# Five engine programs emitted straight into the main body, with no block around them

## The chip, the cores and the metric

The kernel runs on one core of a Trainium2 chip. The metric is device time in microseconds of one execution, as a median of several runs. Each run also has a profile with a *span*: the time from the first to the last recorded instruction of the program. Time minus span is what the execution spends outside the program's own records, before the first and after the last of them. That difference gets a short name here: the *outside time*. Spans of timed runs are given to 0.1 us, so a single outside time is good to about 0.05 us.

The granted clock is the share of its full clock that TensorE was given; it was at least 0.99 in every run quoted, every one of them undisturbed. Ratios and their 95% intervals are those of the record: mean times of fast runs of the same rounds, where some sets enter without their first run, so they are not quite the ratio of the medians or means quoted beside them. Instants to the nanosecond are read from the trace's single records; the views shown here round them to 0.1 or 0.01 us.

## The reference, cut to what matters

```python
def reference(A_x, A_wqkv, A_wo, B_x, B_w_gate, B_w_up, B_w_down, gate_w):
    x = A_x                                             # [1, 2048, 640] bf16
    g = _sigmoid((x * gate_w).sum(-1, keepdims=True))
    a = _A_ref(x, A_wqkv, A_wo)                         # linear attention, 32 heads of 20
    b = _B_ref(x, B_w_gate, B_w_up, B_w_down)           # gelu(x@w_gate) * (x@w_up) @ w_down
    return g * a + (1 - g) * b
```

The change does not touch the arithmetic. What matters is that the work is one long stream of matrix products, followed by the store of the last 128 rows of the result.

## The kernel before

The kernel plans all operations first. Each engine (TensorE `pe`, ScalarE `act`, VectorE `dve`, GpSimd `pool`, SyncE `sp`) has a list of operations with the semaphores (counters by which one engine waits for another or for a transfer) that each waits for. At the end the lists are emitted, one body per engine, inside a block.

```python
    def emit(self, eng, handle):
        for (waits, fn, key, inc) in self.ops[eng]:
            for (k, v) in waits:
                handle.wait_ge(self.sems[k], v)
            inst = fn(handle)
            inst.then_inc(self.sems[key], inc)
# ... (cut)
    with (
        nc.Block() as block,
        nc.sbuf_tensor("pool", [128, TOTAL], BF16) as pool,
# ... (cut: semaphores, tiles, the plan of all operations)
            n_out = P.count["out"]

            @block.sync
            def _(sp):
                P.emit("sp", sp)
                sp.wait_ge(s_out, n_out)      # all output transfers have landed

            @block.tensor
            def _(pe):
                P.emit("pe", pe)
# ... (cut: the same for scalar, vector, gpsimd)
```

The block does two things. Each engine branches into a body of its own and, behind it, to a common end: in the program as built there are ten unconditional branches, two on each engine. When the block is left, all five engines meet in a closing barrier. Each engine drains (a record that, on VectorE, ends just behind the engine's last operation) and reports on one semaphore, GpSimd collects the reports, and then it releases the others. The opening of the program also has such a barrier, which does not belong to the block.

The last tile's output goes out in two transfers, so that the first 512 columns leave while the last 128 are still computed:

```python
                    if end:
                        P.op("sp", lambda e, c0=c0, cn=cn: e.dma_start(
                            out[0, i * 128:(i + 1) * 128, c0:c0 + cn], out_sb[i][:, c0:c0 + cn]),
                            reads=[r_out[i] if n == 0 else r_out_b[i]], dma="out")
```

Of the kernel before, what the change touches and what calls it, by code (L numbers as in the profile page):

```python
# [159 lines left out]
def bass_gated_mix__linear_attn_block__geglu_ffn__prompt_kernel(  # L160
# [59 lines left out]
    n_dma_in = 100  # L220

    with (
        nc.Block() as block,
        nc.sbuf_tensor("pool", [128, TOTAL], BF16) as pool,
        nc.psum_tensor("ps", [128, 8, 512], F32) as ps,
        nc.semaphore("s_pe") as s_pe,
# [5 lines left out]
        with contextlib.ExitStack() as stack:  # L232
            dma_sems = [stack.enter_context(nc.semaphore("s_in%d" % i)) for i in range(n_dma_in)]

            P = _Plan(["pe", "act", "dve", "pool", "sp"])
# [240 lines left out]
            for n in range(2 * NT):  # L476
# [6 lines left out]
                if n == 3:  # L483
                    dma_in(wq[:, :, 0:640], A_wqkv[:, 0:640].rearrange("(k p) w -> p k w", p=128), [r_wq],
                           eng="act")
# [285 lines left out]

            n_out = P.count["out"]

            @block.sync
            def _(sp):
                P.emit("sp", sp)
                sp.wait_ge(s_out, n_out)

            @block.tensor
            def _(pe):  # L780
                P.emit("pe", pe)

            @block.scalar
            def _(act):
                P.emit("act", act)

            @block.vector
            def _(dve):
                P.emit("dve", dve)

            @block.gpsimd
            def _(g):
                P.emit("pool", g)


# [26 lines left out]
```

## Time and profile before

| kernel before, first three runs | |
|---|---|
| time, median | 278.12 us (277.77 to 278.28) |
| profiled run: time, span | 277.85 us, 275.927 us |
| outside time of that run | 1.92 us |
| TensorE busy | 270.1 us, 98% of the span |
| from the start of the last matmul to the end of the last record | 2.660 us |
| from the start of the record that waits for the outputs to the end of the last record | 0.397 us |

These lines of the profile's page give the span, the busy time of the engines (PE is TensorE) and the chain of waits that ended last, by engine:

```profile
span 275.9 us, 4048 instructions
...
PE 270.1 (98%) x1663; PEld 140.4 (51%) x1696; DVE 138.5 (50%) x233; ACT 78.3 (28%) x132; POOL 26.1 (9%) x28
...
PE 95%; DMA 2%; issue 1%; ACTq 1%; DVE 0%
```

TensorE is the bound. A change that leaves its stream alone can act only at the two ends.

The head, from the timeline (columns: start, duration, engine, line, operation, operands; a q behind an engine's name is its instruction queue):

```profile
0.80 0.57 ACTq L331 DMA_DIRECT2D pool<-in_gate_w_dram  x1
...
0.81 0.14 PEld L387 LDWEIGHTS ps<-const-bfloat16-1.0 128*128 128x128 bf16 x2 [0.81 <-issue]
...
3.72 1.28 ACT L441 ACT_TABLE_LOAD   x1 [3.72 <-issue]
```

The opening barrier releases the engines at 0.724 to 0.736 us, and the own work of all but VectorE, which first waits for TensorE until about 4.1 us, starts at 0.80 to 0.81 us. There is no room for anything long between the two.

The tail, as the view of the block's own source line. Columns are the line, engine, operation and count, then the shortest, median and longest duration in ns, then the first and last start in us:

```profile
L223 POOLq EVENT_SEMAPHORE  x2: 17/17/17, 275.7 to 275.8; - x2
L223 POOLq DRAIN  x1: 1512/1512/1512, 165.7 to 165.7; - x1
L223 ACTq DRAIN  x1: 826/826/826, 214.0 to 214.0; - x1
L223 PEldq DRAIN  x1: 1995/1995/1995, 271.5 to 271.5; - x1
L223 DVEq DRAIN  x1: 391/391/391, 273.5 to 273.5; - x1
L223 SPq COMPARE_BRANCH  x1: 38/38/38, 275.5 to 275.5; - x1
L223 SPq DRAIN  x1: 13/13/13, 275.7 to 275.7; - x1
L223 SPq EVENT_SEMAPHORE  x1: 17/17/17, 275.9 to 275.9; - x1
L223 ACTq EVENT_SEMAPHORE  x1: 17/17/17, 275.9 to 275.9; - x1
L223 DVEq EVENT_SEMAPHORE  x1: 21/21/21, 275.9 to 275.9; - x1
L223 PEldq EVENT_SEMAPHORE  x1: 51/51/51, 275.9 to 275.9; - x1
```

This is the whole closing barrier. GpSimd has drained at 167 us and ScalarE at 215 us, TensorE at 273.5 us and VectorE at 273.9 us, and all of them then sit and wait. SyncE arrives last: its wait for the outputs is carried by a compare-and-branch that starts at 275.530 us, and its drain follows at 275.706. Then GpSimd collects and releases, and at about 275.9 us all four others leave the barrier.

### The profile page before, as it was taken

The numbers are of one execution on the slowest core, as the hardware profiler recorded it, in microseconds if no ns is written. First come the engines' busy times: TensorE is split into PE (matmuls) and PEld (weight loads), VectorE is DVE, ScalarE is ACT, GpSimd is POOL, SyncE is SP. The second block draws the span as 40 slices with busy tenths as digits, with TensorE's granted clock in tenths as the row PEclk, the third lists the DMA queues.
The fourth block names the chain that finished last, engine by engine and source line by source line (L and its number), as shares of the span: only waits on it lengthen the run. The fifth ranks groups of instructions, "written<-read, shape, count | busy, mean of one in ns | idle before, by whom it ended". The sixth has DMA issues, their size and how long they took to land.

```text
span 275.9 us, 4048 instructions
## 1 busy us (share of the span) xinstructions
PE 270.1 (98%) x1663; PEld 140.4 (51%) x1696; DVE 138.5 (50%) x233; ACT 78.3 (28%) x132; POOL 26.1 (9%) x28
## 2 busy tenths in 40 slices
PE   8899999999999999999999999999999999999996
PEld 5455555555545444444444444444555555555553
DVE  2398888510234324999999998535000122212223
ACT  1355555210431454223222223224555100000000
POOL 5000000000000401242432422000000000000000
PEclk9999999999999999999999999999999999999999
DMA  7998997002120111122121221380000010111111
GB/s 178 172 199 238 395 402 244 12 6 44 23 48 21 50 46 54 25 46 48 26 49 24 47 50 24 60 309 14 0 0 2 24 47 26 48 50 48 50 48 48
DMA packets 36400, 22.38 MB, mean 81 GB/s; under 512 B 25759, under 2 KB 34975, under 8 KB 36383
## 3 DMA queue, kind: packets, MB, share of 16 engines
q1 hardware_dynamic: 34997, 20.49, 27.4%
q10 hardware_dynamic: 1386, 1.64, 2.2%
q8 instruction: 13, 0.21, 0.3%
q14 instruction: 4, 0.03, 0.0%
HBM read 13.11 MB, written 2.62 MB: 57 GB/s over the span
## 4 chain that ended last, share of the span: by engine, by line
PE 95%; DMA 2%; issue 1%; ACTq 1%; DVE 0%
PE ps L596 41%; PE ps L739 20%; PE ps L702 6%; PE ps L432 6%; PE ps L503 6%; PE ps L419 5%; DMA pool<-in_A_wqkv_dram 2%; PE ps L505 2%; PE ps L433 2%; PE ps L703 2%; PE ps L420 2%; PE ps L571 2%; PE ps L723 1%; ACTq L331 1%; PE ps L617 1%
## 5 line engine op out<-in xcount | busy, mean ns | idle before, releaser
L596 PE MATMUL ps<-pool 128*128 128x512 bf16 x509 | 113.0, 379 | 0.6
L596 PEld LDWEIGHTS ps<-pool 128*128 128x128 bf16 x520 | 50.4, 98 | 60.0 <-issue 0.3
L739 PE MATMUL ps<-pool 128*128 128x128 bf16 (+1 forms) x407 | 56.6, 297 | 0.6 <-issue 0.2
L604 DVE TENSOR_TENSOR pool<-ps,pool 128x512 bf16<-128x512 f32 x52 | 35.8, 688 | 33.6 <-PE ps L596 30.4
L602 ACT ACTIVATE pool<-ps 128x512 f32<-128x512 f32 x52 | 31.1, 597 | 72.5 <-PE ps L596 72.1
L750 DVE SCALAR_TENSOR_TENSOR pool<-ps,pool 128x512 bf16<-128x512 f32 (+1 forms) x32 | 16.2, 547 | 63.8 <-PE ps L739 63.8
L739 PEld LDWEIGHTS ps<-pool 128*128 128x128 bf16 x416 | 31.8, 98 | 25.3 <-issue 1.1
L648 POOL TENSOR_TENSOR pool<-pool 128x640 f32<-128x640 bf16 x16 | 22.5, 1409 | 140.1 <-DMA pool<-z_row 87.1
L441 ACT ACTIVATE pool<-ps 128x640 bf16<-128x640 f32 x32 | 22.3, 704 | 23.1 <-PE ps L420 13.5
L454 DVE SCALAR_TENSOR_TENSOR pool<-ps,pool 128x640 bf16<-128x640 f32 x32 | 26.4, 825 | 2.2
L656 DVE TENSOR_TENSOR pool<-pool 128x640 bf16<-128x640 bf16 x16 | 23.0, 1441 | 0.6
L419 PE MATMUL ps<-pool 128*128 128x512 bf16 x77 | 21.9, 383 | 0.7 <-DMA pool<-in_A_wqkv_dram 0.7
L432 PE MATMUL ps<-pool 128*128 128x512 bf16 x77 | 21.4, 379 | 0.0
L702 PE MATMUL ps<-pool 128*128 128x512 bf16 x77 | 21.3, 379 | 0.0
L503 PE MATMUL ps<-pool 128*128 128x512 bf16 x76 | 21.2, 379 | 0.0
L505 PE MATMUL ps<-pool 128*128 128x129 bf16 x80 | 17.6, 220 | 0.2
L420 PE MATMUL ps<-pool 128*128 128x128 bf16 x80 | 17.6, 220 | 0.2
L433 PE MATMUL ps<-pool 128*128 128x129 bf16 x80 | 17.6, 220 | 0.2
L703 PE MATMUL ps<-pool 128*128 128x128 bf16 x80 | 17.5, 219 | 0.2
L707 ACT ACTIVATE pool<-ps,pool 128x640 f32<-128x640 f32 x16 | 12.7, 794 | 9.2 <-PE ps L703 9.2
L451 DVE TENSOR_SCALAR pool<-pool 128x640 bf16<-128x640 bf16 x32 | 10.4, 325 | 7.4 <-ACT pool L441 5.8
L419 PEld LDWEIGHTS ps<-pool 128*128 128x128 bf16 x80 | 7.9, 98 | 10.2 <-DMA pool<-in_A_wqkv_dram 1.0
(51 smaller groups left out, 130.7 us busy)
## 6 DMA issues: line engine op xcount, KB each, us to landing
out_dram<-pool SPq DMA_DIRECT2D x15, 160.0 KB, 1.8
pool<-in_B_w_gate_dram SPq DMA_DIRECT2D x1, 2080.0 KB, 13.6
pool<-in_B_w_up_dram SPq DMA_DIRECT2D x1, 2080.0 KB, 18.3
pool<-in_A_x_dram SPq DMA_DIRECT2D x1, 1280.0 KB, 8.3
pool<-in_B_w_down_dram SPq DMA_DIRECT2D x1, 1120.0 KB, 6.0
pool<-in_A_wo_dram SPq DMA_DIRECT2D x6, 160.0 KB, 8.8
pool<-in_B_w_down_dram SPq DMA_DIRECT2D x1, 960.0 KB, 8.5
pool<-in_A_wqkv_dram ACTq DMA_DIRECT2D x5, 160.0 KB, 4.4
```

Source lines behind the costliest of these rows:

```text
L419: e.matmul(ps[:, b0, :], lhs, wk[:, k, 0:512], start=(k == 0), stop=(k == KC - 1))
L420: last = e.matmul(ps[:, b1, 0:128], lhs, wk[:, k, 512:640], start=(k == 0), stop=(k == KC - 1))
L432: e.matmul(ps[:, b0, :], lhs, wq[:, k, 0:512], start=(k == 0), stop=(k == KC - 1))
L433: last = e.matmul(ps[:, b1, 0:129], lhs, wq[:, k, 512:641], start=(k == 0), stop=(k == KC - 1))
L454: P.op("dve", lambda e: e.scalar_tensor_tensor(dst, ps_flat[:, b0 * 512:b0 * 512 + 640], 1.0 + EPS, e_buf[m], ALU.add, ALU.max), reads=[ba ...
L503: e.matmul(ps[:, bs[n], :], lhs, x_aug[:, i, 0:512], start=(i == 0), stop=(i == NT - 1))
L505: last = e.matmul(ps[:, bt, n * 129:(n + 1) * 129], lhs, x_aug[:, i, 512:641], start=(i == 0 and n == 0), stop=(i == NT - 1), skip_group_c ...
L596: last = e.matmul(ps[:, b, :], w[:, k, fc * 128:(fc + 1) * 128], xT[:, k, j * 512:(j + 1) * 512], start=(k == 0), stop=(k == KC - 1))
L602: P.op("act", lambda e: e.activation(ge[n], ps[:, gb, :], ACT.Gelu_apprx_tanh), reads=[bank[gb]], writes=[r_ge[n]])
L604: P.op("dve", lambda e: e.tensor_tensor(hT[fc][:, j * 512:(j + 1) * 512], ps[:, ub, :], ge[n], ALU.mult), reads=[bank[ub], r_ge[n]], write ...
L702: e.matmul(ps[:, b0, :], lhs, w2[:, m, 0:512], start=(m == 0), stop=(m == KC - 1))
L739: last = e.matmul(dst, lhs, wd[:, fc, c0:c0 + cn], start=False, stop=(fc == NFC - 2), skip_group_check=True)
```

## The change

The intent is to save the branches and the closing barrier: the programs synchronise by their own semaphores, and SyncE waits for the last output anyway.

```diff
     with (
-        nc.Block() as block,
         nc.sbuf_tensor("pool", [128, TOTAL], BF16) as pool,
...
-            @block.sync
-            def _(sp):
-                P.emit("sp", sp)
-                sp.wait_ge(s_out, n_out)
-
-            @block.tensor
-            def _(pe):
-                P.emit("pe", pe)
-
... (cut: the same for scalar, vector, gpsimd)
+            for eng, handle in (("sp", nc.sync), ("pe", nc.tensor), ("act", nc.scalar),
+                                ("dve", nc.vector), ("pool", nc.gpsimd)):
+                P.emit(eng, handle)
+            nc.sync.wait_ge(s_out, n_out)
```

More of the change, by code (lines that the diff above doesn't have):

```diff
@@ L772, in bass_gated_mix__linear_attn_block__geglu_ffn__prompt_kernel @@
             n_out = P.count["out"]
-            @block.sync
-            def _(sp):
-                P.emit("sp", sp)
-                sp.wait_ge(s_out, n_out)
-            @block.tensor
-            def _(pe):
-                P.emit("pe", pe)
-            @block.scalar
-            def _(act):
-                P.emit("act", act)
-            @block.vector
-            def _(dve):
-                P.emit("dve", dve)
-            @block.gpsimd
-            def _(g):
-                P.emit("pool", g)
+            for eng, handle in (("sp", nc.sync), ("pe", nc.tensor), ("act", nc.scalar),
+                                ("dve", nc.vector), ("pool", nc.gpsimd)):
+                P.emit(eng, handle)
+            nc.sync.wait_ge(s_out, n_out)
 _INS = ['A_x', 'A_wqkv', 'A_wo', 'B_x', 'B_w_gate', 'B_w_up', 'B_w_down', 'gate_w']
```

## The prediction

> What bounds the kernel now. The page's busy table has TensorE at 270.1 of 275.9 us (98%); the next, VectorE, at 50%. The chain that ended last is 95% TensorE, 2% DMA (the key weights at the start). The granted clock is 1.000. So the matmul stream from about 3 us to 273.5 us sets the time, with a short head and tail. The change alters no instruction of that stream: each engine keeps its program, waits and order. Only what stands around the five programs goes.
>
> The head. The trace shows an opening barrier that belongs to the program's start, not to the block: the engines are released at 0.724 to 0.736 us. It stays. From the end of that release to the engine's first own instruction it is 24 ns on TensorE (0.787 to 0.811), 56 ns on ScalarE's queue (0.745 to 0.801), 68 ns on SyncE's queue (0.741 to 0.809). No branch is recorded there. The Trainium skill, "Advanced Engine Details and Errata", section Control Flow Timing, gives about 51 ns for a branch; TensorE's 24 ns leave no room for one, so the branches to the bodies are probably laid out as fall-through. Estimated gain: 0 to 0.05 us, on the path, since the chain starts with ScalarE's weight issues at 0.80 us.
>
> The tail. The last matmul ends at about 273.5, VectorE's last eviction at 273.88; the last output transfer is issued at 273.95 to 274.39. SyncE's wait for the outputs ends at 275.530, recorded as a compare-and-branch of 38 ns that carries the wait. Then comes the block's barrier: SyncE's drain at 275.706 (138 ns behind the branch), GpSimd's collecting wait 275.744, its release 275.823, the other four engines' waits, the last ending at 275.927. The other drains came long before (VectorE's ended at 273.93), so only SyncE's arrival counts. From 275.530 to 275.927 is 0.397 us, all on the path, since nothing runs beside it. In its place stands one plain semaphore wait, 17 ns like SyncE's others. Gain in the span: 0.38 us.
>
> Outside the span. Timed run and span differ by 277.85 - 275.9 = 1.95 us. The Trainium skill, "Runtime: NRT & Kernel Launch", section on the preamble and postamble, says that the runtime puts its own barrier behind each kernel (about 1.5 us); no trace here shows it. It waits for SyncE in either version, so I expect 1.95 us to stay, perhaps a tenth or two less because four engines arrive early.
>
> Predicted time: 278.12 - 0.38 - about 0.04 = 277.7 us; a gain of 0.15%, within the spread of three runs (277.77 to 278.28). Range 277.2 to 278.2. Faster by over 2%: 1%. Within 2%: 98%. Slower by over 2%: 1%.
>
> What would show it. Right: a span of 275.5 +- 0.15; no drain, compare-and-branch or barrier wait behind the last output; all engines' busy times within 0.2 us; the first weight issue still at about 0.80 us. Wrong at the head: first issues more than 0.1 us earlier. Wrong at the tail: the time falls with no change of span, or the span falls and the time does not, so that the runtime's end absorbs the barrier.
>
> What would make it wrong. ScalarE's table load (1.283 us, now at 3.72, behind the weight issues) might be placed differently when all programs share one body: ahead of the issues it would delay the first weights by up to 1.3 us, still under 1%. The compiler could also attach waits to other instructions.

## The result, and the profile after

| first comparison, six runs each | before | after |
|---|---|---|
| time, median | 278.06 us (277.73 to 279.41) | 277.12 us (276.67 to 277.30) |
| ratio, 95% interval | | 0.9957 [0.9936, 0.9979] |
| span of the profiled run | 275.927 us | 275.882 us |
| outside time of the profiled run | 1.92 us | 1.31 us |
| last matmul's start | 273.267 us | 273.608 us |
| from there to the end of the last record | 2.660 us | 2.274 us |

The kernel is 0.94 us faster by the medians: within 2%, as forecast, but more than twice the gain that I had given it, and 0.08 us under the lower end of my range. At the same time the two profiled spans are almost equal. The two traces explain why, once three pieces are kept apart.

*The body.* The page's lines are as before, with 11 records fewer, which are the block's barrier and branch less the new wait:

```profile
span 275.9 us, 4037 instructions
...
PE 269.3 (98%) x1663; PEld 139.6 (51%) x1696; DVE 138.4 (50%) x233; ACT 78.2 (28%) x132; POOL 26.0 (9%) x28
...
PE 95%; DMA 2%; issue 1%; ACTq 1%; DVE 0%
```

From the first query matmul to the last matmul of the kernel the trace of before has 244.641 us, that of after 244.641 us. In all sixteen traces it lies between 244.639 and 244.642 us. The change does nothing there.

*The head.* It starts as before, and the table load did not move:

```profile
0.80 0.57 ACTq L330 DMA_DIRECT2D pool<-in_gate_w_dram  x1
...
0.81 0.14 PEld L386 LDWEIGHTS ps<-const-bfloat16-1.0 128*128 128x128 bf16 x2 [0.81 <-issue]
...
3.72 1.28 ACT L440 ACT_TABLE_LOAD   x1 [3.72 <-issue]
```

But the first query matmul starts at 28.626 us before and at 28.967 us after, 0.34 us later. The waits view says what TensorE waited for (total us, number of waits, longest). Before:

```profile
PEld ps L419 <- DMA pool<-in_A_wqkv_dram: 1.0, 1, 1.0
PE ps L419 <- DMA pool<-in_A_wqkv_dram: 0.7, 1, 0.7
```

After:

```profile
PEld ps L418 <- DMA pool<-in_A_wqkv_dram: 1.6, 1, 1.6
PE ps L418 <- DMA pool<-in_A_wqkv_dram: 1.3, 1, 1.3
```

In this run the key weights landed later, and TensorE waited 1.3 us for them in place of 0.7. The matmul behind this wait starts at 9.04 us before and at 9.38 us after, which is the whole 0.34 us. Is that an effect of the change? Subtract each kernel's traced tail (below) from the spans of its timed runs: what is left, the start of the last matmul, is 273.74 us on average in 42 runs with the block and 273.66 us in 68 runs of all kernels without it (standard errors 0.09 and 0.07). It spreads over more than 2 us in either group, so a difference of 0.34 us between two runs is within chance, and no effect of the block on the head is seen. The stretches of the windows view (columns: stretch, its length, then busy us of PE, PEld, DVE, ACT and POOL with counts, clock, DMA share, GB/s) locate it. Before:

```profile
0.00:10.00 10.00, 8.44 (x49) 4.65 (x50) 1.56 (x4) 1.28 (x1) 3.60 (x12) 1.00 0.88 183
10.00:70.00 60.00, 59.53 (x434) 33.94 (x441) 37.21 (x68) 24.29 (x50) 0.00 (x0) 1.00 0.65 187
...
273.00:276.00 3.00, 0.49 (x9) 0.31 (x6) 0.88 (x2) 0.00 (x0) 0.00 (x0) 0.98 0.18 55
```

After:

```profile
0.00:10.00 10.00, 7.29 (x47) 3.70 (x48) 1.56 (x4) 1.28 (x1) 3.59 (x12) 1.00 0.90 175
10.00:70.00 60.00, 59.53 (x434) 33.91 (x441) 37.21 (x68) 24.28 (x50) 0.00 (x0) 1.00 0.66 188
...
273.00:276.00 3.00, 0.83 (x14) 0.65 (x12) 1.08 (x2) 0.00 (x0) 0.00 (x0) 1.00 0.18 55
```

TensorE's busy time differs in the first 10 us (1.15 us less after) and in the last 3, where five matmuls more are left to do; between 10 and 70 us it is the same to the last digit, and so it is between 70 and 273 us (201.62 us in both).

*The tail.* The only record of the change's own last line is SyncE's wait:

```profile
L776 SPq EVENT_SEMAPHORE  x1: 17/17/17, 275.9 to 275.9; - x1
```

The tail is 0.386 us shorter, as predicted (0.38). It vanishes in the span because the head of this one run came 0.341 us later.

So the predicted saving is there, and what I missed lies elsewhere: outside the span, where 1.92 us had become 1.31. All six timed runs of after have 1.27 to 1.34 us.

### The profile page after: what moved, and what is told of

The parts are those of the page before. It is cut to its first block, busy times and chain, and to the rows that moved or that the text cites. A ratio compares the mean times of both kernels' runs of the same rounds, so it can differ in the third digit from the quotient of the medians.

```text
span 275.9 us, 4037 instructions
## 1 busy us (share of the span) xinstructions
PE 269.3 (98%) x1663; PEld 139.6 (51%) x1696; DVE 138.4 (50%) x233; ACT 78.2 (28%) x132; POOL 26.0 (9%) x28
## 4 chain that ended last, share of the span: by engine, by line
PE 95%; DMA 2%; issue 1%; ACTq 1%; DVE 0%
PE ps L595 41%; PE ps L738 20%; PE ps L431 6%; PE ps L701 6%; PE ps L502 6%; PE ps L418 5%; DMA pool<-in_A_wqkv_dram 2%; PE ps L504 2%; PE ps L432 2%; PE ps L702 2%; PE ps L419 2%; PE ps L570 2%; PE ps L722 1%; ACTq L330 1%; PE ps L616 1%
```

## The experiments

Three theories for the 0.6 us outside the span:

- A, own ends: behind its last instruction each engine has an end of its own that no record shows. An engine that is done early goes through it while the others still work. The closing barrier holds all five back until 275.9 us, and then the longest of the five ends counts.
- B: the barrier's drains and semaphore instructions themselves leave something behind the last record.
- C: the block's branches do.

All kernels below gave correct results. Each was timed beside runs of the kernel before on the same chip; the four sets (e, f, g, h) ran on four different chips, on which the kernel before had 1.87, 1.94, 1.93 and 1.96 us outside. Quoted are means over the runs, with the range of the single runs for the outside time.

### The noise, and the barrier put back in three ways

`e0_before_again` is the kernel before, unchanged.

> The kernel before, unchanged, to have its span beside each time. The time outside the span (timed run minus span) was 1.92 us in its one profiled run; the changed kernel's six runs have 1.27 to 1.34. All theories: 1.9 to 2.0 us in every run here, span 275.6 to 276.5 (it moves with the landing of the first weights), ratio 1.000 +- 0.001. If this gap moves by 0.3 us between runs, the 0.6 us that is unexplained was chance.

`e1_barrier_no_block` has a barrier, but no block:

```diff
             nc.sync.wait_ge(s_out, n_out)
+            nc.all_engine_barrier()
```

> The changed kernel with one all-engine barrier (drains and semaphores) put back behind SyncE's last wait, still no block and no branch. Theory A (the runtime's end begins on each engine when that engine is done, and the barrier holds all five back until 275.9): gap 1.9 to 2.0 us, tail from last matmul to last record about 2.65 us less SyncE's branch, ratio 0.999 to 1.000. Rival C (the branches of the block, at the head before the first record or at the end behind the last one, cost the 0.6 us): gap 1.3 us, time about 277.5.

`e2_all_wait_no_barrier` has neither, but all five engines end at the same time:

```diff
             nc.sync.wait_ge(s_out, n_out)
+            nc.tensor.wait_ge(s_out, n_out)
+            nc.scalar.wait_ge(s_out, n_out)
+            nc.vector.wait_ge(s_out, n_out)
+            nc.gpsimd.wait_ge(s_out, n_out)
```

> The changed kernel in which the four other engines also wait for the last output, each for itself: no barrier, no drain, no branch, but all five come to their end at the same time. Theory A (late arrival of the other engines at the runtime's end): gap 1.8 to 2.0 us with a tail about 0.38 us shorter than before, so ratio about 0.9985, time 277.6 to 277.7. Rival B (the barrier's own drains and semaphore instructions leave 0.6 us behind the last record): gap 1.3 us, time as the changed kernel's, ratio 0.996.

`e3_sem_barrier_no_block` has the barrier without drains:

```diff
             nc.sync.wait_ge(s_out, n_out)
+            nc.all_engine_barrier(sem_only=True)
```

> As e1, with the barrier made of semaphores alone, without drains. Theory A: gap 1.9 to 2.0 us as in e1, since the engines are as late; tail within 0.2 us of e1's. Rival B in the form 'the drains cost it': gap 1.3 us here and 1.9 in e1.

| run (6 runs each) | ratio to before, 95% | mean time | mean span | outside time | tail in the trace |
|---|---|---|---|---|---|
| before, in the same rounds (11) | | 278.22 | 276.35 | 1.87 (1.74 to 1.99) | |
| e0_before_again | 1.0013 [0.9987, 1.0039] | 278.55 | 276.67 | 1.88 (1.80 to 1.98) | 2.660 |
| e1_barrier_no_block | 1.0002 [0.9975, 1.0030] | 278.25 | 276.37 | 1.89 (1.71 to 1.98) | 2.555 |
| e2_all_wait_no_barrier | 1.0002 [0.9979, 1.0025] | 278.24 | 276.30 | 1.93 (1.78 to 2.07) | 2.325 |
| e3_sem_barrier_no_block | 0.9986 [0.9963, 1.0008] | 277.79 | 275.88 | 1.91 (1.77 to 2.06) | 2.483 |

The tail is from the start of the last matmul to the end of the last record. e0 shows the noise: its spans run from 275.7 to 277.7 us, while its outside times stay within 0.2 us. Therefore the verdict rests on the outside time and the tail, and not on the ratios, whose intervals are as wide as the effect. Some expectations missed for the same reason: e0's runs did not all lie in the stated 1.9 to 2.0 us and 275.6 to 276.5 us, and e2 was expected at 277.6 to 277.7 us and a ratio of 0.9985, but had 278.24 us and 1.0002. Its outside time (1.93 us) and its tail (0.34 us shorter than before) were about as theory A had them.

Theory C falls by e1: with no branch at all the outside time is back at 1.89 us. Theory B falls by e2 and e3: without barrier and drains, with nothing but one wait per engine for the last output, it is 1.93 us; with semaphores alone, 1.91. What the three have in common is that all engines end late, as three of e2's five waits show (SyncE, GpSimd, TensorE):

```profile
L776 SPq EVENT_SEMAPHORE  x1: 17/17/17, 276.3 to 276.3; - x1
...
L780 POOLq EVENT_SEMAPHORE  x1: 17/17/17, 276.3 to 276.3; - x1
...
L777 PEldq EVENT_SEMAPHORE  x1: 51/51/51, 276.3 to 276.3; - x1
```

e2 also shows that this does not pass through the span: its tail is only 0.05 us longer than after's, and its outside time 0.6 us.

SyncE's branch at the end does have a small cost, in the span. Here are e1's wait for the outputs, and the lines of its barrier that answer to SyncE's drain and last wait in the view of before:

```profile
L776 SPq EVENT_SEMAPHORE  x1: 17/17/17, 275.8 to 275.8; - x1
L777 SPq DRAIN  x1: 13/13/13, 275.8 to 275.8; - x1
L777 SPq EVENT_SEMAPHORE  x1: 17/17/17, 276.0 to 276.0; - x1
```

In e1 SyncE's wait starts at 275.769 us and its drain at 275.833, 64 ns later. Before, with the branch between them, it was 275.530 to 275.706, 176 ns (169 in e0). The branch at the end cost 112 ns; the tails differ by 0.105 us. The Trainium skill, "Advanced Engine Details and Errata", section Control Flow Timing, gives about 108 ns for a compare-and-branch; this trace agrees, although the record itself shows only 38 ns.

### One engine late beside SyncE

In each of these four runs one more engine waits for the last output, for instance:

```diff
             nc.sync.wait_ge(s_out, n_out)
+            nc.tensor.wait_ge(s_out, n_out)
```

> The changed kernel with SyncE and TensorE both waiting for the last output; ScalarE, VectorE and GpSimd end early. Time outside the span, against 1.30 us with SyncE alone and 1.93 with all five late. A1 (each engine ends at the runtime's own pace and the slowest of those that are late counts): one of the four runs of this call has 1.8 to 2.0 us and engines that end as fast as SyncE have 1.3. A2 (engines that end together share something, so each late one adds a part): each run has about 1.30 + 0.6/4 = 1.45 us.

> As f1 with ScalarE as the second late engine. A1: 1.3 us, or 1.8 to 2.0 if ScalarE is the slow one. A2: about 1.45 us.

> As f1 with VectorE as the second late engine. A1: 1.3 us, or 1.8 to 2.0 if VectorE is the slow one (its sequencer records are the slower ones, 21 ns against 17 for a semaphore wait, so it is a candidate). A2: about 1.45 us.

> As f1 with GpSimd as the second late engine. A1: 1.3 us, or 1.8 to 2.0 if GpSimd is the slow one. A2: about 1.45 us.

### One engine late instead of SyncE

In these four the final wait is moved from SyncE to another engine, for instance:

```diff
-            nc.sync.wait_ge(s_out, n_out)
+            nc.tensor.wait_ge(s_out, n_out)
```

> The changed kernel with the final wait for the outputs on TensorE instead of SyncE; the other four, SyncE too, end early. Time outside the span: if an engine's own end sets it, the value is that engine's own: 1.8 to 2.0 us for an engine whose f run had that, and at most 1.30 us for one whose f run had 1.3. If SyncE has a longer end than the others, a value under 1.30 us shows it, and that kernel would beat the changed one.

> As g1 with the final wait on ScalarE, which has nothing to do after 215 us. Own-end theory: at most 1.30 us if f2 had 1.3, else f2's value.

> As g1 with the final wait on VectorE. Own-end theory: at most 1.30 us if f3 had 1.3, else f3's value.

> As g1 with the final wait on GpSimd, which has nothing to do after 167 us. Own-end theory: at most 1.30 us if f4 had 1.3, else f4's value.

Both sets (four runs each; before had 1.94 us outside in the rounds of the f set and 1.93 in those of the g set):

| last engine | f: with SyncE, outside time | f: ratio, 95% | g: alone, outside time | g: ratio, 95% |
|---|---|---|---|---|
| TensorE | 1.57 (1.54 to 1.60) | 0.9954 [0.9927, 0.9980] | 1.56 (1.54 to 1.60) | 0.9982 [0.9963, 1.0000] |
| ScalarE | 1.60 (1.55 to 1.67) | 0.9970 [0.9949, 0.9992] | 1.61 (1.37 to 1.75) | 0.9972 [0.9957, 0.9987] |
| VectorE | 1.40 (1.36 to 1.43) | 0.9969 [0.9941, 0.9996] | 1.55 (1.39 to 1.96) | 0.9967 [0.9947, 0.9986] |
| GpSimd | 2.06 (1.80 to 2.31) | 0.9990 [0.9963, 1.0016] | 1.86 (1.81 to 1.88) | 0.9981 [0.9962, 1.0000] |
| SyncE (the changed kernel, 6 runs) | | | 1.30 (1.27 to 1.34) | 0.9957 [0.9936, 0.9979] |

A2, in which each late engine adds a part and every f run has about 1.45 us, falls: the four differ by up to 0.66 us. A1 holds: the time depends on which engine is late, and it is the same within 0.04 us whether SyncE is late with it or not (for VectorE and GpSimd only without the single runs that are named below). GpSimd has the longest end, about 1.87 us (the median of g4), and alone accounts for the 1.9 us that all five together show. A part of A1's wording missed: I had expected one slow engine and four like SyncE. In fact the ends are graded: SyncE 1.30, VectorE 1.40, TensorE 1.57, ScalarE 1.60, GpSimd 1.87 us. These are whole outside times; the part of them that lies before the first record is not known, so only their differences belong to the ends. SyncE's value comes from other chips than the f and g sets, and the kernel before differs by up to 0.09 us between chips, so the steps from SyncE to VectorE and from TensorE to ScalarE are hardly clear of the noise; the others are.

Single runs stand outside the pattern: two of f4 at 2.27 and 2.31 us, one of g3 at 1.96 (its other three have 1.39 to 1.44), one of g2 at 1.37. I have no cause for them. They do not change the order of the engines, except that f4's mean is above g4's.

No g set has a shorter mean outside time than the changed kernel, so SyncE is the right engine to end on. No version was found that clearly beats it (f1's ratio of 0.9954 is the same within the noise).

One rival to theory A stays. If the engines met in a fixed order behind the program, and a late engine held back all that come behind it in that order, the same graded times would be seen without any engine having a longer end. No run here tells the two apart. What is shown is that the outside time is set by which engines are late.

### A barrier without GpSimd

So far everything pointed to late engines, but no run had had a barrier without GpSimd in it. The changed kernel was also timed again beside it.

> The changed kernel once more, with five rounds. All theories: 1.27 to 1.34 us outside the span; ratio 0.9965 +- 0.001 (0.38 us of the span and 0.60 us outside it, of 278.2).

```diff
             nc.sync.wait_ge(s_out, n_out)
+            E = mybir.EngineType
+            nc.multi_engine_barrier([E.SP, E.PE, E.Activation, E.DVE])
```

> The changed kernel with a closing barrier of SyncE, TensorE, ScalarE and VectorE; GpSimd is left out of it and ends early. Own-end theory (the slowest of the late engines counts; GpSimd 1.87, ScalarE 1.6, TensorE 1.57, VectorE 1.4, SyncE 1.3 us): 1.55 to 1.65 us outside the span though a barrier is there. Rival (a barrier of any membership costs 0.6 us behind the last record): 1.85 to 1.95 us. Tail within 0.2 us of the 2.56 us that the barrier of five without the block has.

| run (6 runs each) | ratio to before, 95% | median | outside time | tail in the trace |
|---|---|---|---|---|
| before, in the same rounds (11) | | 277.97 | 1.96 (1.83 to 2.05) | |
| h1_after_again | 0.9969 [0.9937, 1.0000] | 277.31 | 1.33 (1.30 to 1.37) | 2.282 |
| h2_barrier_of_four | 0.9990 [0.9954, 1.0027] | 277.64 | 1.66 (1.62 to 1.72) | 2.530 |

The view of h2's barrier line, where ScalarE now does the collecting and no GpSimd record stands:

```profile
L778 ACTq EVENT_SEMAPHORE  x2: 17/17/17, 275.7 to 275.8; - x2
...
L778 SPq DRAIN  x1: 13/13/13, 275.7 to 275.7; - x1
...
L778 PEldq EVENT_SEMAPHORE  x1: 51/51/51, 275.8 to 275.8; - x1
```

The barrier costs as much of the span as the one of five (tail 2.530 against 2.555 us), but outside the span it is 1.66 us, close to the ends of ScalarE and TensorE (1.60 and 1.57). It is slightly above the expected 1.55 to 1.65, and far from 1.9. So it is not a barrier as such that costs outside time; it is which engines it makes late.

## Why the prediction was wrong

Point by point:

- *What bounds the kernel, and that its stream would not change*: right. The stretch from the first query matmul to the last matmul is 244.64 us in every trace.
- *Head, 0 to 0.05 us*: nothing was found. The first weight issue is at 0.80 us in both traces, and in e1, which has the barrier but no branches, every engine's first own instruction after the opening starts within 0.02 us of its time before. The skill's 51 ns for a branch was used to rule a branch out, and no run shows one there; the program compiled again has none there either.
- *Tail, 0.38 us*: right. It measured 0.386 us between the first two traces and 0.378 between e0 and h1. Its parts: the branch 0.105 us (before against e1), the barrier 0.28 us (e1 against after).
- *A span of 275.5 +- 0.15 us as the mark of a right tail*: badly chosen, and so was "the time falls with no change of span" as the mark of a wrong one, which is what the first two profiles showed. The head moves the whole span by chance: the first query matmul starts anywhere between 28.35 and 29.81 us in the sixteen traces, which is several times the effect. The profiled span of after, 275.88, looked like a failure although the tail was just as predicted. A time from the last matmul on would have been the right mark. "All busy times within 0.2 us" failed for TensorE (270.1 against 269.3); that difference, too, arises in the first 10 us.
- *The table load might move, the compiler might attach waits differently*: neither happened. The load is at 3.72 us in both.
- *Outside the span, "I expect 1.95 us to stay, perhaps a tenth or two less because four engines arrive early"*: this is the step that failed. The sentence in front of it, "It waits for SyncE in either version", has the flaw. SyncE is the last to arrive in both versions, but before the change the other four were released at the same moment, and the time is then the one that GpSimd, when late, shows alone (1.86 us in g4), not SyncE's 1.30. The direction was named, and the size was wrong: 1.92 us (mean of 36 runs of before) became 1.30 and 1.33 us (six runs each), a gain of 0.6 us in place of 0.1 to 0.2. In the sum itself only 0.04 us had been entered for everything but the tail. That the first median, 277.12 us, fell below the range and the second, 277.31 us in h1, inside it lies within the chance of the head; the 0.6 us is there both times.

With this term mended the sum is 0.38 + 0.6 = 1.0 us, or 0.36% of 278.2 us. Measured were 0.94 and 0.66 us by medians, and ratios of 0.9957 and 0.9969, in whose intervals 0.9964 lies both times. What the head's chance adds or takes in a given set of runs is larger than what is left over.

What stays open: what the engines do behind their last records, why GpSimd's share is the longest, and whether each engine has an end of its own or the order in which they meet decides. The Trainium skill, "Runtime: NRT & Kernel Launch", section "The ~15µs preamble/postamble breakdown", lists a barrier for all engines and resets of semaphores behind the kernel; no record of these traces lies behind the program's last instruction, so no run here shows which of that work an engine does before it meets the others.

## What to carry to other kernels

Here the closing barrier did not only cost its own records (0.28 us): it made every engine late, and the execution then had the outside time of its slowest engine (1.87 us) instead of that of SyncE (1.30 us). One kernel on one core shows this, and the gain is about a third of a per cent. Let each engine finish when its own work is done, and put the one final wait on the engine with the shortest end (SyncE here). When a change acts at an end of the program, compare time minus span and a stretch counted from a fixed event, not whole spans whose start moves by chance.

## What the Trainium skill lacked or had wrong

- "Runtime: NRT & Kernel Launch", the preamble and postamble table: it gives one time for each stage behind a kernel and does not say that the engine which ends last matters. The runs show that the time outside the program depends on which engine ends last: 1.30 us for SyncE, 1.40 for VectorE, about 1.57 for TensorE, 1.6 for ScalarE and 1.87 for GpSimd, and that an engine which ends early does not add its share.
- No page says what a block around the engine programs costs: here 0.38 us in the span (a branch of 0.105 and a barrier of 0.28 us) and 0.6 us outside it.
- "Advanced Engine Details and Errata", Control Flow Timing: its 108 ns for a compare-and-branch agree with the 112 ns that the branch added between SyncE's wait and its drain. What it lacks is that the branch's record shows only 38 ns.
